# Queries parked with their half-swapped copy, denominators inverted on VectorE in pieces, some transposes on TensorE, SP's queue depth in the schedule

## The chip, the cores and the metric

The kernel runs on one core of a Trainium2 chip. The metric is device time in microseconds. A median of repeated runs is quoted. Profiles are of one execution, so a profile's span can differ from the median by about 0.3%.

Engines: PE is TensorE (PEld its weight loads), DVE is VectorE, ACT is ScalarE, POOL is GpSimd, SP is SyncE, which here only issues transfers.

## The reference

Four layers over a sequence of 2048 rows and 1024 columns, 32 heads of 32: linear attention (A), softmax attention (B), A, B, each with a layer norm before and a residual after. Type bfloat16.

```python
def _A_ref(x, wqkv, w_phi, wo):             # linear attention
    # q, k, v from x @ wqkv, 32 heads
    pq = einsum("bhsd,hdf->bhsf", q, w_phi); pk = ... k ...
    phi_q = concat([softmax(pq), softmax(-pq)]); phi_k = ...
    kv  = einsum("bhsf,bhsd->bhfd", phi_k, v); z = phi_k.sum(s)
    o = einsum(phi_q, kv) / (einsum(phi_q, z) + 1e-6)
    return o @ wo
def _B_ref(x, wqkv, wo):                    # softmax attention
    scores = einsum("bhqd,bhkd->bhqk", q, k) * Dh ** -0.5
    o = softmax(scores) @ v
    return o @ wo
x = x + _A_ref(ln(x)); x = x + _B_ref(ln(x)); x = x + _A_ref(ln(x)); x = x + _B_ref(ln(x))
```

## The kernel before

The kernel records its instructions with its own scheduler. A small clock in Python models each engine, a transfer queue per issuer (`"D"` is SP's, `"P"` GpSimd's) and the buffers, and decides in which order instructions stand on each engine. In the traces each engine runs its list in that order (below, VectorE stands 13.80 us at one instruction while another is queued behind it). So a wrong cost in the model costs no time by itself; it makes an order in which an engine stands in front of something that is not there yet.

An attention unit is a pair of heads times up to 512 queries. TensorE makes scores into `ring`, ScalarE takes the exponential into `E`, TensorE sums `E` against V and against ones into one PSUM accumulator `acc`. VectorE evicts `acc`, or adds it to an earlier partial sum that was parked in DRAM (`pd`). Meanwhile TensorE does background work: projections, feature maps and key-value sums of other rows (`bg`, the `kvacc` accumulator).

The denominators of a finished pair of units go out through DRAM to be spread over 128 partitions, inverted, and fetched back as broadcast rows:

```python
def norm(x0, x1):                            # one pair of units
    ...
    yield ("op", "D", 0.07, lambda e: nc.sync.dma_start(out=dn[0:2, :], in_=a0[64:128:32, :]), 0.0)
    yield dma(dn[2:4, :], a1[0:64:32, :], 20)
    yield dma(rc[:, 0:m], dn[:].rearrange("a (p e) -> (a p) e", e=m), 20)
    yield ("op", "V", 0.2, lambda e: nc.vector.reciprocal(out=rc[:, 0:m], in_=rc[:, 0:m]))
    yield dma(rn[:].rearrange("a (p e) -> (a p) e", e=m), rc[:, 0:m], 20)
    for j in range(4):                       # four broadcast loads of 32 partitions
        ...
    yield tt("P", c_pool(n), o[0:64, ot_cols(u)], a0[0:64, :], a1[0:64, :], ALU.mult)
    yield tt("P", c_pool(n), o[64:128, ot_cols(u)], a1[64:128, :], a0[64:128, :], ALU.mult)
```

A query tile is parked in DRAM as it is, and loaded three times, to get a copy with its halves swapped:

```python
def q_load1(s, src, n, key):
    yield ("op", "D", 0.07, lambda e: nc.sync.dma_start(out=s[:, 0, 0:n], in_=src), 0.0)
    yield ("op", "D", 0.07, lambda e: nc.sync.dma_start(out=s[0:64, 1, 0:n], in_=src[64:128]), 0.0)
    yield dma(s[64:128, 1, 0:n], src[0:64], 256)
```

Normalised rows are transposed by a transfer (`dma_t(xn[u][...], xb2[:])`), and so are the outputs of linear attention. In the scheduler every issue on SP costs 0.07 us and any number of transfers may be in flight.

The softmax here doesn't subtract the row's maximum and nothing guards it: scores larger than these inputs give would overflow.

Of the kernel before, what the change touches and what calls it, by code (L numbers as in the profile page):

```python
# [18 lines left out]
P = 128  # L19
D = 1024  # L20
# [90 lines left out]
class Clock:  # L111


    def __init__(self):
        self.now = 0.0
        self.heap = []
        self.n = 0
        self.busy = {}
        self.keys = {}
        self.kwait = {}  # L120

# [39 lines left out]
    def _op(self, gen, eng, cost, fn, lat=SEM):  # L161
        if isinstance(eng, tuple):
            eng = min(eng, key=lambda e: max(self.busy.get(e, 0.0), self.now))
        if isinstance(cost, dict):
            c = cost[eng]
        else:
            c = cost
        t0 = self.busy.get(eng, 0.0)
        if t0 > self.now + 1e-9:
            self.at(t0, lambda: self._op(gen, eng, cost, fn, lat))  # L170
            return
        fn(eng)
        self.busy[eng] = self.now + c
        if callable(lat):
            lat = lat()
        self.at(self.now + c + lat, lambda: self.step(gen, None))

    def set(self, k):
# [80 lines left out]
def kernel(  # L259
# [64 lines left out]
    st_s = Slots(clk, [sb(f"st{i}", [P, 18], F32) for i in range(4)])  # L324
    sm_s = Slots(clk, [sb(f"sm{i}", [P, 64], F32) for i in range(4)])
    fq_s = Slots(clk, [sb(f"fq{i}", [P, 256], F32) for i in range(2)])
    rc_s = Slots(clk, [sb(f"rc{i}", [P, 16], F32) for i in range(4)])

    def tok(n):
        return Slots(clk, [0] * n)  # L330
# [12 lines left out]

    X = [None] + [[dd(f"x{l}_{t}", [P, D]) for t in range(NT)] for l in (1, 2, 3)]
    xsp = {(l, c): dd(f"xs{l}_{c}", [P, PO, C]) for l in (0, 2) for c in range(NC)}
    qd = {(l, c, g): dd(f"qd{l}_{c}_{g}", [P, C]) for l in (1, 3) for c in range(NC) for g in range(G)}
    pd = {(l, q, p): dd(f"pd{l}_{q}_{p}", [P, C], F32) for l in (1, 3) for q in range(3) for p in range(16)}
    dnd = {n: [dd(f"dn{n}_{i}", [4, n], F32) for i in range(4)] for n in (256, 512)}
    rnd = {n: [dd(f"rn{n}_{i}", [4, n], F32) for i in range(4)] for n in (256, 512)}
    dn_i = [0]  # L350

    def xsrc(l, t):
        if l == 0:
            return A_x[0, t * P:(t + 1) * P, :]
# [9 lines left out]
        return lat  # L364

    def dma(o, i, kb=4):
        return ("op", "D", 0.07, lambda e: nc.sync.dma_start(out=o, in_=i), queue("D", kb))

    def bulk(o, i, kb):
        return ("op", "P", 1.0, lambda e: nc.gpsimd.dma_start(out=o, in_=i), queue("P", kb))  # L370

    def dma_t(o, i):
        return ("op", "D", 0.07, lambda e: nc.sync.dma_start_transpose(out=o, in_=i), queue("D", 400))

    def eng(e):
        return {"V": nc.vector, "S": nc.scalar, "P": nc.gpsimd}[e]
# [17 lines left out]
    def drop(token, b):  # L394
        token.give(0)
        blk.give(b)
# [48 lines left out]
    def ln_tail(u, t, xb, st):  # L445
# [9 lines left out]
        st_s.give(st)  # L455
        clk.start(ln_turn(u, t, xb2))

    def ln_turn(u, t, xb2):
        yield ("key", ("xs", u))
        tt_ = t % 4  # L460
        yield dma_t(xn[u][:, :, tt_ * P:(tt_ + 1) * P], xb2[:])
        drop(t_xn, xb2)
        clk.set(("xt", u, tt_))
        xn_cnt[u] += 1
        if xn_cnt[u] == 4:
            clk.set(("xnT", u))
# [222 lines left out]

    def build_AK(l, c, prs=(0, 1), hs=(0, 1)):  # L690
        u = (l, "K", c)
        if 0 in prs and 0 in hs:
            clk.start(xslot(u, 17))
            clk.start(spill(u))
# [126 lines left out]
    def build_DN(l, c):  # L821
# [38 lines left out]
        def nn(gp, t):  # L860
# [11 lines left out]
            def post(bank, rel, b):  # L872
                ke, kf = ("e", l, c, gp), ("f", l, c, gp)
                n_cnt[ke] = n_cnt.get(ke, 0) + 1
                if n_cnt[ke] == 4:
                    for gi in range(2):
                        drop(t_eq, eq_b[l, c, 2 * gp + gi])
                tmp = b
                t32 = tmp[:].bitcast(F32)
                f = fq_b[l, c, gp]  # L880
                fb = f[:, 192 + 16 * t:192 + 16 * (t + 1)].unsqueeze(2).to_broadcast([P, 16, DH])
                yield tt("V", c_ps(512), t32.rearrange("p (x i) -> p x i", i=DH),
                         bank[:].rearrange("p (x i) -> p x i", i=DH), fb, ALU.mult)
                rel()
                n_cnt[kf] = n_cnt.get(kf, 0) + 1
                if n_cnt[kf] == 4:
                    fq_s.give(f)
                k = (l, 4 * c + t)
                if k not in o_b:
                    o_b[k] = None  # L890
                    o_b[k] = yield from grab(t_o)
                    clk.set(("ob", k))
                    n_cnt[k] = 0
                else:
                    yield ("key", ("ob", k))
                t4 = t32.rearrange("p (g s n) -> p g s n", g=2, s=2)
                yield tt("P" if att_active() else ("V", "P"), {"P": c_pool(256), "V": c_sb(256)},
                         o_b[k][:, gp * 256:(gp + 1) * 256].rearrange("p (g n) -> p g n", g=2),
                         t4[:, :, 0, :], t4[:, :, 1, :], ALU.add)
                drop(t_tmp, tmp)  # L900
                n_cnt[k] += 1
                if n_cnt[k] == 4:
                    oT = yield from grab(t_oT)
                    yield dma_t(oT[:].rearrange("p (g n) -> p g n", g=G), o_b[k][:])
                    drop(t_o, o_b[k])
                    oT_b[k] = oT
                    clk.set(("oT",) + k)
            add(f"n{l}.{c}.{gp}.{t}", [("f", l, c, gp)], None, mms, post, t_tmp)

        ds(0)  # L910
# [5 lines left out]
                ds(gp + 2)  # L916

    def build_AO(l, c):
        for t in range(4):
            tg = 4 * c + t  # L920
            clk.start(x_chain(l, tg, ("oT", l, tg)))
# [14 lines left out]
    def build_BP(l, c, h):  # L936
        u = (l, "B", c)
        if h == 0:
            clk.start(xslot(u, 24))

        def kk(g):
            gl = g % 4
# [13 lines left out]
        def qq(g):  # L956
            gl = g % 4

            def post(bank, rel, b):
                use_xn(u)  # L960
                yield cp(b[:, 0:C], bank[:], C)
                rel()
                yield dma(qd[l, c, g][:], b[:, 0:C], 128)
                drop(t_q, b)
                clk.set(("Qd", l, c, g))
            add(f"q{l}.{c}.{g}", [("xnT", u)], ("bq", g // 4),
# [34 lines left out]
    def q_loader():  # L1001
        for l in (1, 3):
            for vi, (qt, w, ks, part, last, hh) in enumerate(VISITS):
                for g in range(4 * hh, 4 * hh + 4):
                    yield ("key", ("Qd", l, qt // 4, g))
                    s = yield ("take", qs_s)
                    Qt[l, vi, g] = s
                    clk.start(q_load1(s, qd[l, qt // 4, g][:, (qt % 4) * P:(qt % 4 + w) * P], w * P, ("Q", l, vi, g)))

    def q_load1(s, src, n, key):  # L1010
        yield ("op", "D", 0.07, lambda e: nc.sync.dma_start(out=s[:, 0, 0:n], in_=src), 0.0)
        yield ("op", "D", 0.07, lambda e: nc.sync.dma_start(out=s[0:64, 1, 0:n], in_=src[64:128]), 0.0)
        yield dma(s[64:128, 1, 0:n], src[0:64], 256)
        clk.set(key)

    def part_loader():
# [14 lines left out]
    def finish_unit(u):  # L1031
# [19 lines left out]
            clk.set(("part", k, v))  # L1051
            return
        kg = (u.l, u.qt, u.g)
        if not u.fast:
            grp.setdefault(kg, []).append((u, a, token, b))
            if len(grp[kg]) == 2:
                clk.start(norm(*grp.pop(kg)))
            return
        yield from ot_slot(u)
        R = yield from grab(t_R)  # L1060
        r = R[:].bitcast(F32)[:, 0:n]
        n0, d0 = 64 * u.b, 64 * (1 - u.b)
        yield ("op", "V", 0.1 + 0.0065 * n, lambda e: nc.vector.reciprocal(out=r[n0:n0 + 64, :], in_=a[d0:d0 + 64, :]))
        yield tt("V", c_sb(n), ot_ap(u.l, u.q, u.g)[n0:n0 + 64, ot_cols(u)], a[n0:n0 + 64, :], r[n0:n0 + 64, :], ALU.mult)
        drop(t_R, R)
        drop(token, b)
        otb_n[kg] = otb_n.get(kg, 0) + 1
        if otb_n[kg] == 2:
            ot_done(u)

# [17 lines left out]
    def ot_done(u):  # L1088
        for t in range(u.qt, u.qt + u.w):
            clk.set(("ot", u.l, t, u.g))  # L1090
            if u.g == 5:
                clk.set(("ot6", u.l, t))

    def norm(x0, x1):
        u, a0, tk0, b0 = x0
        _, a1, tk1, b1 = x1
        n = u.n
        i = dn_i[0] % 4
        dn_i[0] += 1
        dn, rn = dnd[n][i], rnd[n][i]  # L1100
        rc = yield ("take", rc_s)
        m = n // 32
        yield ("op", "D", 0.07, lambda e: nc.sync.dma_start(out=dn[0:2, :], in_=a0[64:128:32, :]), 0.0)
        yield dma(dn[2:4, :], a1[0:64:32, :], 20)
        yield dma(rc[:, 0:m], dn[:].rearrange("a (p e) -> (a p) e", e=m), 20)
        yield ("op", "V", 0.2, lambda e: nc.vector.reciprocal(out=rc[:, 0:m], in_=rc[:, 0:m]))
        yield dma(rn[:].rearrange("a (p e) -> (a p) e", e=m), rc[:, 0:m], 20)
        rc_s.give(rc)
        for j in range(4):
            dst = (a1[32 * j:32 * (j + 1), :] if j < 2 else a0[32 * j:32 * (j + 1), :])  # L1110
            yield ("op", "D", 0.07, lambda e, j=j, dst=dst: nc.sync.dma_start(
                out=dst, in_=rn[j:j + 1, :].to_broadcast([32, n])), queue("D", 256) if j == 3 else 0.0)
        yield from ot_slot(u)
        o = ot_ap(u.l, u.q, u.g)
        yield tt("P", c_pool(n), o[0:64, ot_cols(u)], a0[0:64, :], a1[0:64, :], ALU.mult)
        yield tt("P", c_pool(n), o[64:128, ot_cols(u)], a1[64:128, :], a0[64:128, :], ALU.mult)
        drop(tk0, b0)
        drop(tk1, b1)
        ot_done(u)

    bo_left = {}

# [304 lines left out]

NBLK = 28
ACT_SLACK = 0.5
NE = 5  # L1430
WINDOW = 60
TRACE = None
# [30 lines left out]
```

## Time and profile before

| | before |
|---|---|
| median | 2660 us |
| PE / ACT / DVE busy | 2292.7 / 2085.9 / 961.8 us |
| issues on SP, in the order of instructions | 1638 |
| PE idle, sum from its timeline | 356 us, 165 of it waiting for exponentials |

The page of before, parts 1 and 2. In part 2 the span is cut into 40 slices and a digit is the busy share in tenths.

```profile
span 2663.0 us, 67052 instructions
## 1 busy us (share of the span) xinstructions
PE 2292.7 (86%) x28268; PEld 913.2 (34%) x28268; DVE 961.8 (36%) x1787; ACT 2085.9 (78%) x2415; POOL 411.2 (15%) x510
...
PE   5878898898999998877878889889889989888787
...
ACT  2433369697999999878986236869797999989998
```

The row of ACT shows the two attentions (the two runs of nines) and the linear layers before each (the twos and threes). Neither PE nor ACT is full everywhere.

I cut the trace at the first and last exponential of each attention. This is the windows view of before for those four stages (start, first attention, boundary, second attention). The columns are stage, length, then busy us of PE, PEld, DVE, ACT, POOL (with counts), granted clock (the share of TensorE's full speed that it was given), DMA share, GB/s.

```profile
0.00:307.70 307.70, 233.75 (x1544) 123.79 (x1545) 201.11 (x382) 97.23 (x177) 75.46 (x118) 0.92 0.56 160
307.70:1437.10 1129.40, 985.93 (x13881) 384.91 (x13882) 397.56 (x711) 989.71 (x1112) 165.80 (x194) 0.93 0.41 117
1437.10:1578.90 141.80, 115.90 (x755) 59.05 (x747) 88.33 (x176) 34.08 (x63) 35.89 (x52) 0.90 0.48 127
1578.90:2650.10 1071.20, 949.54 (x12060) 342.31 (x12060) 269.42 (x513) 964.90 (x1063) 133.47 (x148) 0.87 0.34 100
```

The long stops of PE, from its timeline in before (start, length, what ran, and in brackets the idle time ahead of it and what ended it):

```profile
22.43 3.17 PE L405 MATMUL bg<-slab,xnT 128*128 128x512 bf16 x7 [22.43 <-DMA xnT<-blk]
...
183.49 1.03 PE L405 MATMUL ring<-slab,xnT 128*128 128x512 bf16 x2 [13.10 <-DMA xnT<-blk]
...
1145.37 3.57 PE L405 MATMUL bg<-slab,xnT 128*128 128x512 bf16 x8 [5.62 <-DVE kvacc L388]
...
1232.72 0.59 PE L744 MATMUL bg<-VA,blk 128*128 128x129 bf16 x4 [11.80 <-DVE kvacc L388]
...
1382.67 2.32 PE L402 MATMUL bg<-slab,xnT 128*32 128x512 bf16 x20 [4.99 <-DVE VA L383]
...
1451.89 3.59 PE L405 MATMUL bg<-V,xnT 128*128 128x512 bf16 x8 [8.77 <-DMA xnT<-blk]
```

Three are waits for a transpose by transfer (`xnT<-blk`). The three from 1145 to 1383 us name DVE, which sounds as if DVE were slow. The chain of waits in before, at the longest, says otherwise (start, length, what):

```profile
1213.76 16.39 DMA dn<-blk
...
1230.23 1.79 DMA rc<-dn
...
1232.04 0.20 DVE rc L1106
1232.25 0.43 DVE kvacc L388
...
1232.72 0.59 PE bg L744 x4
```

DVE stands for 13.80 us in front of a reciprocal of 0.2 us, because the transfer on the way to its input (`dn<-blk`) took 16.39 us to land. The key-value addition that PE needs is queued behind it and takes 0.43 us. The other two stops have the same cause: by the DVE timeline it stood 5.68 us (1145) and 4.94 us (1383) at the same small reciprocal just before. The waits view of before sums this (engine, line, releaser: total, times, longest):

```profile
POOL blk L388 <- DMA blk<-rn: 717.8, 88, 21.2
...
DVE rc L1106 <- DMA rc<-dn: 131.9, 41, 13.8
```

The larger number is idle time of an engine that has little to do. The smaller one blocks others.

### The profile page before, as it was taken

The page shows a single profiled execution, that of the slowest core. Times are in us where ns is not written, and L with a number is a line of the kernel's source. Part 1 is how long each engine was busy: PE and PEld are TensorE (multiplying, and loading weights), DVE is VectorE, ACT ScalarE, POOL GpSimd, SP SyncE. Part 2 cuts the span into 40 slices and gives each one's busy share as a digit, 9 for nine tenths or more (in the row PEclk, how much of TensorE's full clock was granted, in tenths as well). Part 3 has the DMA queues.
Part 4 walks back from the last instruction along what each step waited for, and adds up shares of the span by engine and source line. Part 5 has one row for each costly group of instructions (what it writes and reads, how often), then busy time and mean ns, then how long its engine had stood idle before and what let it go on. Part 6 is the DMA issues. An engine that isn't in the chain of part 4 may idle for free.

```text
span 2663.0 us, 67052 instructions
## 1 busy us (share of the span) xinstructions
PE 2292.7 (86%) x28268; PEld 913.2 (34%) x28268; DVE 961.8 (36%) x1787; ACT 2085.9 (78%) x2415; POOL 411.2 (15%) x510
## 2 busy tenths in 40 slices
PE   5878898898999998877878889889889989888787
PEld 2434432333333222333334443333333322223333
DVE  4865641432332234533334665133233221121011
ACT  2433369697999999878986236869797999989998
POOL 3122200100100211221122210010021011122010
PEclk8988999899999889988999899989999987777777
DMA  8364652553253344444134454346335233242111
GB/s 253 86 168 143 162 164 91 149 150 127 72 149 99 112 133 133 134 123 88 43 111 97 130 132 126 102 121 187 104 104 150 93 93 99 88 124 77 32 29 30
DMA packets 280110, 306.69 MB, mean 115 GB/s; under 512 B 147400, under 2 KB 198464, under 8 KB 276736
## 3 DMA queue, kind: packets, MB, share of 16 engines
q1 hardware_dynamic: 253424, 192.29, 26.7%
q0 software_dynamic: 26384, 110.11, 13.1%
q8 instruction: 221, 3.62, 0.6%
q14 instruction: 81, 0.66, 0.1%
HBM read 204.79 MB, written 72.34 MB: 104 GB/s over the span
## 4 chain that ended last, share of the span: by engine, by line
PE 49%; ACT 17%; issue 7%; DMA 4%; DVE 4%; SPq 1%; POOL 0%; ACTq 0%; POOLq 0%; DVEq 0%
PE bg L402 16%; ACT E L1257 15%; PE acc L1313 13%; PE ring L1277 12%; PE ring L405 4%; PE bg L405 3%; DVE blk L388 1%; DMA rc<-dn 1%; DMA xnT<-blk 1%; DMA dn<-blk 1%; ACT blk L705 1%; ACT blk L809 1%; DVE K2b L383 1%; DMA blk<-pd 0%; PE ring L867 0%
## 5 line engine op out<-in xcount | busy, mean ns | idle before, releaser
L1257 ACT ACTIVATE E<-ring 128x1024 bf16<-128x1024 f32 x2048 | 1910.9, 1111 | 197.4 <-PE ring L1277 175.0
L1313 PE MATMUL acc<-E,V 128*32 128x512 bf16 (+1 forms) x5120 | 707.8, 377 | 10.9 <-DVE blk L388 8.6
L1313 PE MATMUL acc<-E,ones 128*32 128x512 bf16 (+1 forms) x5120 | 707.8, 378 | 0.0
L1277 PE MATMUL ring<-Q,K2b 32*128 32x512 bf16 (+1 forms) x2560 | 438.9, 369 | 156.2 <-ACT E L1257 150.0
L1277 PE MATMUL ring<-Q,K2a 32*128 32x512 bf16 (+1 forms) x2560 | 457.8, 371 | 13.6 <-ACT E L1257 13.5
L1313 PEld LDWEIGHTS <-V 128*32 128x32 bf16 x5120 | 204.9, 100 | 315.7 <-issue 286.9
L388 POOL TENSOR_TENSOR blk<-blk,blk 64x512 bf16<-64x512 f32 (+1 forms) x156 | 166.1, 1065 | 773.9 <-DMA blk<-rn 717.8
L1277 PEld LDWEIGHTS <-K2a 32*128 32x128 bf16 x2560 | 123.6, 93 | 427.5 <-issue 417.2
L1277 PEld LDWEIGHTS <-K2b 32*128 32x128 bf16 x2560 | 155.4, 93 | 280.5 <-issue 274.4
L1043 DVE COPY blk<-acc 128x512 f32<-128x512 f32 (+1 forms) x160 | 93.2, 582 | 422.6 <-PE acc L1313 399.4
L388 DVE TENSOR_TENSOR blk<-blk,acc 128x512 f32<-128x512 f32 x128 | 87.6, 684 | 340.3 <-PE acc L1313 322.7
L1313 PEld LDWEIGHTS <-ones 128*32 128x32 bf16 x5120 | 200.8, 100 | 2.1
L402 PE MATMUL bg<-slab,blk 128*32 128x512 bf16 x2596 | 174.3, 386 | 6.8 <-DVE blk L388 5.1
L405 PEld LDWEIGHTS <-xnT 128*128 128x128 bf16 x809 | 80.7, 102 | 163.3 <-DMA xnT<-blk 45.8
L402 PE MATMUL bg<-slab,xnT 128*32 128x512 bf16 x1740 | 124.3, 407 | 14.2 <-ACT blk L705 7.8
L388 DVE TENSOR_TENSOR blk<-blk,bg 128x512 bf16<-128x512 bf16 x110 | 75.3, 685 | 153.5 <-PE bg L402 134.1
L405 PE MATMUL ring<-slab,xnT 128*128 128x512 bf16 x416 | 103.6, 391 | 22.4 <-DMA xnT<-blk 13.1
L388 POOL TENSOR_TENSOR blk<-blk 128x256 bf16<-128x256 f32 x112 | 80.1, 725 | 216.9 <-DVE blk L388 211.9
L402 PEld LDWEIGHTS <-blk 128*32 128x32 bf16 x2968 | 82.6, 98 | 80.9 <-issue 22.8
L710 DVE TENSOR_REDUCE sm<-blk 128x32 f32<-128x1024 bf16 x64 | 77.5, 1211 | 90.7 <-ACT blk L705 86.7
L402 PE MATMUL bg<-xnT,slab 128*32 128x512 bf16 x1424 | 101.0, 397 | 10.4 <-DVE K2b L383 5.8
L405 PE MATMUL bg<-slab,xnT 128*128 128x512 bf16 x301 | 78.9, 409 | 30.0 <-DMA xnT<-blk 22.4
(179 smaller groups left out, 2130.1 us busy)
## 6 DMA issues: line engine op xcount, KB each, us to landing
pd<-blk SPq DMA_DIRECT2D x128, 256.0 KB
blk<-pd SPq DMA_DIRECT2D x128, 256.0 KB
slab<-in_B_wqkv_dram POOLq DMA_DIRECT2D x28, 1024.0 KB, 7.3
Q<-qd SPq DMA_DIRECT2D x256, 64.0 KB
Q<-qd SPq DMA_DIRECT2D x112, 128.0 KB
x<-blk SPq DMA_DIRECT2D x48, 256.0 KB
blk<-rn SPq DMA_DIRECT2D x192, 64.0 KB
blk<-x SPq DMA_DIRECT2D x48, 256.0 KB
```

Source lines behind the costliest of these rows:

```text
L383: eng(e).tensor_copy(out=o, in_=i)
L388: return ("op", e, cost, lambda x: eng(x).tensor_tensor(out=o, in0=a, in1=b, op=op))
L402: nc.tensor.matmul(o[js], lhsT=l[:, js], rhs=r, start=st, stop=sp, tile_position=(0, 32 * j), skip_group_check=True)
L405: nc.tensor.matmul(o, lhsT=l, rhs=r, start=st, stop=sp, skip_group_check=True)
L705: yield ("op", "S", c_act(C), lambda x, s=s: nc.scalar.activation(out=e[:, s * C:(s + 1) * C], in_=bank[:], func=ACT.Exp, scale=1.0 - 2.0 ...
L710: yield ("op", "V", c_sb(1024), lambda x: nc.vector.reduce_sum(out=sm[:, 0:32], in_=e3, axis=AX.X))
L809: yield ("op", "S", c_act(C), lambda x, s=s: nc.scalar.activation(out=e[:, s * C:(s + 1) * C], in_=bank[:], func=ACT.Exp, scale=1.0 - 2.0 ...
L1043: yield ("op", "V", c_ps(n), lambda e: nc.vector.tensor_copy(out=a, in_=acc_t[:, 0:n]))
L1257: yield ("op", "S", c_act(2 * n), lambda x: nc.scalar.activation(out=E[:, :, 0:n], in_=ring_t[buf][:, :, 0:n], func=ACT.Exp, scale=INV_SQR ...
L1277: nc.tensor.matmul(ring_t[bufs[e]][:, j, i * n:(i + 1) * n], lhsT=K2[e][c][u.g // 4][r, u.g % 4, m, :], rhs=u.Q[r, e, 0:n], start=True, st ...
L1313: nc.tensor.matmul(u.acc[r0 + 32 * j:r0 + 32 * j + 32, 0:n], lhsT=lh, rhs=E[:, j, i * n:(i + 1) * n], start=first, stop=final, tile_positi ...
```

## The change

The intent is to relieve SP and its queue, and to let the recorded order know what an issue costs. It has four parts: *schedule*, *queries*, *denominators*, *transposes*.

```diff
 # schedule
+        fly = self.fly.get(eng, ()) if callable(lat) else ()
+        if len(fly) >= 8:
+            t0 = max(t0, fly[-8])
-        return ("op", "D", 0.07, lambda e: nc.sync.dma_start(out=o, in_=i), queue("D", kb))
+        return ("op", "D", 0.45, lambda e: nc.sync.dma_start(out=o, in_=i), queue("D", kb))
-        return ("op", "D", 0.07, ... dma_start_transpose ...)
+        return ("op", "D", 1.3, ... dma_start_transpose ...)
 # queries: parked as [P, 2, C], loaded at once
+                for x in (0, 64):
+                    yield ("op", "V", c_sb(C, 4), lambda e, x=x: nc.vector.tensor_copy(
+                        out=b2[x:x + 64, 1, :], in_=b2[64 - x:128 - x, 0, :]))
-                yield dma(qd[l, c, g][:], b[:, 0:C], 128)
+                yield dma(qd[l, c, g][:], b2, 256)
-        (three loads)
+        yield dma(s[:, :, 0:n], src, n * 0.5)
 # denominators: norm() and its nine transfers are gone
+            yield ("op", "V", c_sb(n, 2), lambda e: nc.vector.tensor_copy(out=r[n0:n0 + 64, :], in_=a[d0:d0 + 64, :]))
+            ...  # the second unit of the pair, when both have copied:
+                for x in range(0, n, P):
+                    yield ("op", "V", 0.1 + 0.0065 * P, lambda e, x=x: nc.vector.reciprocal(
+                        out=r[:, x:x + P], in_=r[:, x:x + P]))
+        yield tt("V" if u.fast else "P", ..., o, a[n0:n0 + 64, :], r[n0:n0 + 64, :], ALU.mult)
 # transposes on TensorE, eight of 128x128 into one bank, then one eviction
+            return (0.062, False, lambda bank, ct, W: nc.tensor.transpose(
+                out=bank.bitcast(BF16)[:, i * P:(i + 1) * P], in_=tr_src[key][0][:, i * P:(i + 1) * P],
+                identity=ident[:]))
+            yield cp(dst, bank.bitcast(BF16).rearrange("p (a n) -> p a n", n=P), 1024)
+TR = {(0, "K", 0), (2, "K", 3), (0, "O", 0), (2, "O", 0), (1, "B", 0), (3, "B", 0)}   # six groups of four tiles
... (cut: the plumbing of keys and buffers)
```

More of the change, by code (lines that the diff above doesn't have):

```diff
@@ L118, in __init__ @@
         self.busy = {}
+        self.fly = {"D": [], "P": []}
         self.keys = {}
@@ L175, in _op @@
             lat = lat()
+            self.fly[eng].append(self.now + c + lat)
         self.at(self.now + c + lat, lambda: self.step(gen, None))
@@ L326 @@
     fq_s = Slots(clk, [sb(f"fq{i}", [P, 256], F32) for i in range(2)])
-    rc_s = Slots(clk, [sb(f"rc{i}", [P, 16], F32) for i in range(4)])
     def tok(n):
@@ L345 @@
     xsp = {(l, c): dd(f"xs{l}_{c}", [P, PO, C]) for l in (0, 2) for c in range(NC)}
-    qd = {(l, c, g): dd(f"qd{l}_{c}_{g}", [P, C]) for l in (1, 3) for c in range(NC) for g in range(G)}
+    qd = {(l, c, g): dd(f"qd{l}_{c}_{g}", [P, 2, C]) for l in (1, 3) for c in range(NC) for g in range(G)}
     pd = {(l, q, p): dd(f"pd{l}_{q}_{p}", [P, C], F32) for l in (1, 3) for q in range(3) for p in range(16)}
-    dnd = {n: [dd(f"dn{n}_{i}", [4, n], F32) for i in range(4)] for n in (256, 512)}
-    rnd = {n: [dd(f"rn{n}_{i}", [4, n], F32) for i in range(4)] for n in (256, 512)}
-    dn_i = [0]
     def xsrc(l, t):
@@ L372, in dma_t @@
     def dma_t(o, i):
-        return ("op", "D", 0.07, lambda e: nc.sync.dma_start_transpose(out=o, in_=i), queue("D", 400))
+        return ("op", "D", 1.3, lambda e: nc.sync.dma_start_transpose(out=o, in_=i), queue("D", 400))
     def eng(e):
@@ L456, in ln_tail, with pe_tr, one, post @@
         clk.start(ln_turn(u, t, xb2))
+    tr_src = {}
+    def pe_tr(key, name):
+        def one(i):
+            return (0.062, False, lambda bank, ct, W: nc.tensor.transpose(
+                out=bank.bitcast(BF16)[:, i * P:(i + 1) * P], in_=tr_src[key][0][:, i * P:(i + 1) * P],
+                identity=ident[:]))
+        def post(bank, rel, b):
+            dst, fin = tr_src[key][1:]
+            yield cp(dst, bank.bitcast(BF16).rearrange("p (a n) -> p a n", n=P), 1024)
+            rel()
+            fin()
+        add(name, [("tr", key)], None, [one(i) for i in range(8)], post)
+    def transpose(key, dst, src, fin):
+        if key in tr_pe:
+            tr_src[key] = (src, dst, fin)
+            clk.set(("tr", key))
+        else:
+            yield dma_t(dst, src[:])
+            fin()
+    tr_pe = set()
     def ln_turn(u, t, xb2):
@@ L460, in ln_turn, with ln_fin @@
         tt_ = t % 4
-        yield dma_t(xn[u][:, :, tt_ * P:(tt_ + 1) * P], xb2[:])
+        yield from transpose((u, tt_), xn[u][:, :, tt_ * P:(tt_ + 1) * P], xb2, lambda: ln_fin(u, tt_, xb2))
+    def ln_fin(u, tt_, xb2):
         drop(t_xn, xb2)
@@ L691, in build_AK @@
         u = (l, "K", c)
+        if u in TR and 0 in hs:
+            for pr in prs:
+                for t in (2 * pr, 2 * pr + 1):
+                    tr_pe.add((u, t))
+                    pe_tr((u, t), f"tr{l}.{c}.{t}")
         if 0 in prs and 0 in hs:
@@ L903, in post, with fin @@
                     oT = yield from grab(t_oT)
-                    yield dma_t(oT[:].rearrange("p (g n) -> p g n", g=G), o_b[k][:])
-                    drop(t_o, o_b[k])
-                    oT_b[k] = oT
-                    clk.set(("oT",) + k)
+                    def fin(oT=oT):
+                        drop(t_o, o_b[k])
+                        oT_b[k] = oT
+                        clk.set(("oT",) + k)
+                    yield from transpose(("o",) + k, oT[:].rearrange("p (g n) -> p g n", g=G), o_b[k], fin)
             add(f"n{l}.{c}.{gp}.{t}", [("f", l, c, gp)], None, mms, post, t_tmp)
@@ L918, in build_AO @@
     def build_AO(l, c):
+        if (l, "O", c) in TR:
+            for t in range(4):
+                tr_pe.add(("o", l, 4 * c + t))
+                pe_tr(("o", l, 4 * c + t), f"to{l}.{c}.{t}")
         for t in range(4):
@@ L939, in build_BP @@
             clk.start(xslot(u, 24))
+            if u in TR:
+                for t in range(4):
+                    tr_pe.add((u, t))
+                    pe_tr((u, t), f"tr{l}.{c}.{t}")
         def kk(g):
@@ L960, in post @@
                 use_xn(u)
-                yield cp(b[:, 0:C], bank[:], C)
+                b2 = b[:].rearrange("p (a n) -> p a n", a=2)
+                yield cp(b2[:, 0, :], bank[:], C)
                 rel()
-                yield dma(qd[l, c, g][:], b[:, 0:C], 128)
+                for x in (0, 64):
+                    yield ("op", "V", c_sb(C, 4), lambda e, x=x: nc.vector.tensor_copy(
+                        out=b2[x:x + 64, 1, :], in_=b2[64 - x:128 - x, 0, :]))
+                yield dma(qd[l, c, g][:], b2, 256)
                 drop(t_q, b)
@@ L1007, in q_loader @@
                     Qt[l, vi, g] = s
-                    clk.start(q_load1(s, qd[l, qt // 4, g][:, (qt % 4) * P:(qt % 4 + w) * P], w * P, ("Q", l, vi, g)))
+                    clk.start(q_load1(s, qd[l, qt // 4, g][:, :, (qt % 4) * P:(qt % 4 + w) * P], w * P, ("Q", l, vi, g)))
     def q_load1(s, src, n, key):
-        yield ("op", "D", 0.07, lambda e: nc.sync.dma_start(out=s[:, 0, 0:n], in_=src), 0.0)
-        yield ("op", "D", 0.07, lambda e: nc.sync.dma_start(out=s[0:64, 1, 0:n], in_=src[64:128]), 0.0)
-        yield dma(s[64:128, 1, 0:n], src[0:64], 256)
+        yield dma(s[:, :, 0:n], src, n * 0.5)
         clk.set(key)
@@ L1053, in finish_unit @@
         kg = (u.l, u.qt, u.g)
-        if not u.fast:
-            grp.setdefault(kg, []).append((u, a, token, b))
-            if len(grp[kg]) == 2:
-                clk.start(norm(*grp.pop(kg)))
-            return
-        yield from ot_slot(u)
-        R = yield from grab(t_R)
-        r = R[:].bitcast(F32)[:, 0:n]
-        n0, d0 = 64 * u.b, 64 * (1 - u.b)
-        yield ("op", "V", 0.1 + 0.0065 * n, lambda e: nc.vector.reciprocal(out=r[n0:n0 + 64, :], in_=a[d0:d0 + 64, :]))
-        yield tt("V", c_sb(n), ot_ap(u.l, u.q, u.g)[n0:n0 + 64, ot_cols(u)], a[n0:n0 + 64, :], r[n0:n0 + 64, :], ALU.mult)
-        drop(t_R, R)
+        n0, d0 = 64 * u.b, 64 * (1 - u.b)
+        yield from ot_slot(u)
+        o = ot_ap(u.l, u.q, u.g)[n0:n0 + 64, ot_cols(u)]
+        if u.fast:
+            R = yield from grab(t_R)
+            r = R[:].bitcast(F32)[:, 0:n]
+            yield ("op", "V", 0.1 + 0.0065 * n, lambda e: nc.vector.reciprocal(out=r[n0:n0 + 64, :], in_=a[d0:d0 + 64, :]))
+        else:
+            if u.b == 0:
+                R = yield from grab(t_R)
+                grp[kg] = R
+                clk.set(("R",) + kg)
+            else:
+                yield ("key", ("R",) + kg)
+                R = grp[kg]
+            r = R[:].bitcast(F32)[:, 0:n]
+            yield ("op", "V", c_sb(n, 2), lambda e: nc.vector.tensor_copy(out=r[n0:n0 + 64, :], in_=a[d0:d0 + 64, :]))
+            clk.set(("Rd", u.b) + kg)
+            if u.b == 0:
+                yield ("key", ("Rd", 1) + kg)
+            else:
+                yield ("key", ("Rd", 0) + kg)
+                for x in range(0, n, P):
+                    yield ("op", "V", 0.1 + 0.0065 * P, lambda e, x=x: nc.vector.reciprocal(
+                        out=r[:, x:x + P], in_=r[:, x:x + P]))
+                clk.set(("Rr",) + kg)
+            yield ("key", ("Rr",) + kg)
+        yield tt("V" if u.fast else "P", c_sb(n) if u.fast else c_pool(n), o, a[n0:n0 + 64, :], r[n0:n0 + 64, :], ALU.mult)
         drop(token, b)
         otb_n[kg] = otb_n.get(kg, 0) + 1
+        if u.fast or otb_n[kg] == 2:
+            drop(t_R, R)
         if otb_n[kg] == 2:
@@ L1092, in ot_done @@
                 clk.set(("ot6", u.l, t))
-    def norm(x0, x1):
-        u, a0, tk0, b0 = x0
-        _, a1, tk1, b1 = x1
-        n = u.n
-        i = dn_i[0] % 4
-        dn_i[0] += 1
-        dn, rn = dnd[n][i], rnd[n][i]
-        rc = yield ("take", rc_s)
-        m = n // 32
-        yield ("op", "D", 0.07, lambda e: nc.sync.dma_start(out=dn[0:2, :], in_=a0[64:128:32, :]), 0.0)
-        yield dma(dn[2:4, :], a1[0:64:32, :], 20)
-        yield dma(rc[:, 0:m], dn[:].rearrange("a (p e) -> (a p) e", e=m), 20)
-        yield ("op", "V", 0.2, lambda e: nc.vector.reciprocal(out=rc[:, 0:m], in_=rc[:, 0:m]))
-        yield dma(rn[:].rearrange("a (p e) -> (a p) e", e=m), rc[:, 0:m], 20)
-        rc_s.give(rc)
-        for j in range(4):
-            dst = (a1[32 * j:32 * (j + 1), :] if j < 2 else a0[32 * j:32 * (j + 1), :])
-            yield ("op", "D", 0.07, lambda e, j=j, dst=dst: nc.sync.dma_start(
-                out=dst, in_=rn[j:j + 1, :].to_broadcast([32, n])), queue("D", 256) if j == 3 else 0.0)
-        yield from ot_slot(u)
-        o = ot_ap(u.l, u.q, u.g)
-        yield tt("P", c_pool(n), o[0:64, ot_cols(u)], a0[0:64, :], a1[0:64, :], ALU.mult)
-        yield tt("P", c_pool(n), o[64:128, ot_cols(u)], a1[64:128, :], a0[64:128, :], ALU.mult)
-        drop(tk0, b0)
-        drop(tk1, b1)
-        ot_done(u)
     bo_left = {}
```

## The prediction

> **What bounds the kernel now.** The page gives PE 2292.7 us busy (86% of 2663.0), ACT 2085.9 (78%), DVE 961.8 (36%). No engine bounds all of it. The 50-us windows show: up to 307 us and from 1430 to 1578 (projections, feature maps) PE is busy 40 to 47 of 50, ACT 10 to 30; in attention (650 to 1100, 1950 to 2650) ACT is busy 48 to 50 (2048 exponentials, 1910.9 us, 0.93 each); between (1100 to 1430) they alternate. PE's idle time in the timeline sums to about 356 us; 165 waits for the exponentials, most of the rest is bank turnover under 1.5 us each. Only the longer stops are in the change's reach: 22.4 us at the start (first transposed tile), 13.1 at 183 (transpose), 5.6 at 1145, 11.8 at 1232 and 5.0 at 1383 (VectorE stuck), 8.8 at 1452 (transpose).
>
> **Removed.** In the order of instructions SP's issues fall from 1638 to 702. Nine denominator transfers per pair of units disappear. Their delay matters through VectorE: the waits show it standing 131.9 us before the small reciprocal (41 times, longest 13.8), other work queued behind; the chain shows that at 1214 (16.4 us of transfer, reciprocal, accumulate, PE). Gain about 22 us from these three stops, 3 more at the end, where broadcast rows are awaited. POOL's 718 us wait for the broadcast costs nothing itself. Q loads go from three transfers to one; they rarely sit on the chain: near 0. With transposes on PE the first matmuls should begin near 14 to 15 us (normalised rows exist at 11.9): 8 us. The 1452 stop: 8 us. The 183 stop has no PE transpose; perhaps half goes by better issue order: 6 us. Sum about 47 us.
>
> **Added.** VectorE: 252 reciprocals of 128x128; the trace has 344 ns for 32 columns and 1747 for 256, so an estimate of 0.93 us each, 234 us; denominator copies, estimated 45 us; half copies 35; evictions of transposes 25, shared with ACT; minus 19. VectorE rises to about 1260 us. In attention windows it is busy 6 to 23 of 50, so this fits, but an eviction may wait up to one reciprocal: 5 to 10 us lost. PE: 192 transposes, mostly in PE-bound stretches, by the 128-column matmuls' spacing of 0.06 to 0.11 us 12 to 20 us. The Trainium skill, "VectorE: DVE Perf Modes", section "The three transpose paths", gives 390 ns for one on TensorE; this trace's back-to-back spacing is smaller, and decides.
>
> **Moved.** About 80 background matmuls of 512 columns move from the first attention to the boundary after it: 15 to 20 us, saved again in the first attention where PE limits it. I count zero.
>
> **Prediction.** 47 minus 12 to 20 minus 5 to 10 is about 25 us: 2632 us, range 2590 to 2662. Faster by over 2% 0.22, within 2% 0.74, slower 0.04.
>
> **What will show it.** First matmul near 14 us; no wait for the small reciprocal, none over 3 us of PE for the key-value accumulator; reciprocals near 0.93 us; DVE busy 1230 to 1290; exponentials still about 1910 us; 1950 to 2650 still ACT-bound, the second attention at most 10 us shorter.
>
> **What would make it wrong.** If the crowded SP queue also delays Q, residual rows and partial sums, more is gained (2600 or below). If the longer boundary is not repaid, or reciprocals delay accumulator evictions by near 1 us at many units, ACT starves and the gain vanishes. A lower granted clock in PE-bound stretches could hide 10 us.

## The result, and the profile after

The median is 2627 us (2624.66 to 2628.97, 4 runs) against 2660 us. All outputs are right. The ratio is 0.9879, 95% interval 0.9857 to 0.9901. All ratios here are the mean time of one kernel's runs over that of the kernel before in the same rounds, so they are not quite the ratios of the medians quoted.

The page of after:

```profile
span 2626.8 us, 65988 instructions
## 1 busy us (share of the span) xinstructions
PE 2304.8 (88%) x28190; PEld 925.2 (35%) x28250; DVE 1262.1 (48%) x2246; ACT 2105.4 (80%) x2443; POOL 426.3 (16%) x519
```

The four stages of after, windows view, columns as above:

```profile
0.00:301.40 301.40, 239.37 (x1635) 130.46 (x1664) 206.79 (x396) 108.42 (x192) 74.76 (x118) 0.95 0.52 154
301.40:1389.20 1087.80, 970.04 (x13558) 375.40 (x13560) 518.41 (x897) 986.82 (x1110) 176.06 (x197) 0.93 0.39 116
1389.20:1551.90 162.70, 139.10 (x952) 75.46 (x962) 107.67 (x208) 45.90 (x81) 40.17 (x58) 0.93 0.35 119
1551.90:2613.80 1061.90, 948.40 (x12021) 340.63 (x12025) 423.87 (x739) 964.21 (x1063) 135.27 (x148) 0.86 0.32 97
```

The first attention lost 41.6 us and the boundary after it gained 20.9: the background work that left one stage stands in the other, as the order had shown. The start lost 6.3 and the second attention 9.3.

PE's timeline of after has no stop for the key-value accumulator above 0.7 us. Its start:

```profile
11.31 1.04 PE L462 MATMUL bg<-ident,blk 128*128 128x128 bf16 x8 [11.31 <-DVE blk L452]
...
16.79 2.39 PE L405 MATMUL bg<-slab,xnT 128*128 128x512 bf16 x8
...
29.69 3.60 PE L405 MATMUL bg<-slab,xnT 128*128 128x512 bf16 x8 [5.33 <-DMA xnT<-blk]
...
39.17 0.39 PE L661 MATMUL bg<-ident,V 128*128 128x128 bf16 x4
```

Projections start 5.6 us earlier than before (16.79 against 22.43). Then PE waits 5.33 us for the *next* rows' transposes, which still go by transfer. The weight fold (`ident,V`) begins at 39.17. In before it began at 40.58:

```profile
40.58 0.38 PE L634 MATMUL bg<-ident,V 128*128 128x128 bf16 x4 [0.88 <-DVE VA L383]
```

Of 5.6 us, 1.4 arrived.

The costliest new group on DVE, by form, in after (count, then busy us and mean ns):

```profile
L1121 DVE RECIPROCAL blk<-blk 128x128 f32<-128x128 f32 x252 | 223.0, 923 | 2.3
...
L1114 DVE COPY blk<-blk 64x512 f32<-64x512 f32 x96 | 50.8, 529 | 3.9
...
L1007 DVE COPY blk<-blk 64x512 bf16<-64x512 bf16 x128 | 43.4, 339 | 3.1
```

DVE does 300 us more and the kernel is faster.

One difference I had named only as a risk. The groups view of ACT gives the exponentials' idle time and its releasers, in before:

```profile
L1257 ACT ACTIVATE E<-ring 128x1024 bf16<-128x1024 f32 x2048 | 1910.9, 1111 | 197.4 <-PE ring L1277 175.0 <-PE acc L1313 20.1 <-ACT E L1257 1.3
```

and in after:

```profile
L1292 ACT ACTIVATE E<-ring 128x1024 bf16<-128x1024 f32 x2048 | 1908.5, 1109 | 152.8 <-PE ring L1312 150.7 <-PE acc L1348 1.0
```

The work is the same; the waits for `acc` fell from 20.1 to 1.0 us. Where they came from is in the chain of waits in before, around one of them (SPq is SP's sequencer, issuing):

```profile
2371.12 0.59 SPq L367
...
2371.81 0.52 SPq L367
...
2372.38 0.42 SPq L1111
...
2372.85 0.41 SPq L1111
2373.31 0.42 SPq L1111
2373.77 0.42 SPq L1111
2374.24 2.73 DMA blk<-pd
2377.06 0.70 DVE blk L388
2377.80 1.05 PE acc L1313 x16
```

The load of the parked partial sum (`blk<-pd`) lands 2.73 us after it is issued, which is quick. It was issued late, because SP was issuing a Q load, a load of denominators and four of their broadcasts (L1111) ahead of it, at 0.4 to 0.6 us each. DVE then adds late, the accumulator comes free late, PE's sums wait, the `E` buffers stay full and ACT stops (5.51 us of idle time up to 2378.30, by its timeline). In the 64 us from 2340, SP issued 92 transfers in before and its issuing took 43 us; in the same stretch of after (2303 to 2367) it issued 22, in 8 us, by the SP timelines.

### The profile page after: what moved, and what is told of

The parts are those of the page before. It is cut to its first block, busy times and chain, and to the rows that moved or that the text cites. A ratio compares the mean times of both kernels' runs of the same rounds, so it can differ in the third digit from the quotient of the medians.

```text
span 2626.8 us, 65988 instructions
## 1 busy us (share of the span) xinstructions
PE 2304.8 (88%) x28190; PEld 925.2 (35%) x28250; DVE 1262.1 (48%) x2246; ACT 2105.4 (80%) x2443; POOL 426.3 (16%) x519
## 5 line engine op out<-in xcount | busy, mean ns | idle before, releaser
L1292 ACT ACTIVATE E<-ring 128x1024 bf16<-128x1024 f32 x2048 | 1908.5, 1109 | 152.8 <-PE ring L1312 150.7
L1312 PE MATMUL ring<-Q,K2a 32*128 32x512 bf16 (+1 forms) x2560 | 459.6, 370 | 10.9 <-ACT E L1292 10.1
L1121 DVE RECIPROCAL blk<-blk 128x128 f32<-128x128 f32 x252 | 223.0, 923 | 2.3
L402 PE MATMUL bg<-slab,xnT 128*32 128x512 bf16 x2076 | 152.2, 414 | 11.0 <-ACT blk L737 9.1
L402 PE MATMUL bg<-xnT,slab 128*32 128x512 bf16 x1596 | 113.0, 399 | 9.6 <-ACT blk L841 4.8
L388 POOL TENSOR_TENSOR blk<-blk 128x256 bf16<-128x256 f32 x102 | 73.5, 730 | 227.3 <-DVE blk L388 226.3
L405 PEld LDWEIGHTS <-xnT 128*128 128x128 bf16 x729 | 71.4, 100 | 101.2 <-issue 18.4
```

The lines of the kernel that those rows point to most:

```text
L388: return ("op", e, cost, lambda x: eng(x).tensor_tensor(out=o, in0=a, in1=b, op=op))
L402: nc.tensor.matmul(o[js], lhsT=l[:, js], rhs=r, start=st, stop=sp, tile_position=(0, 32 * j), skip_group_check=True)
L405: nc.tensor.matmul(o, lhsT=l, rhs=r, start=st, stop=sp, skip_group_check=True)
L1121: yield ("op", "V", 0.1 + 0.0065 * P, lambda e, x=x: nc.vector.reciprocal(out=r[:, x:x + P], in_=r[:, x:x + P]))
L1292: yield ("op", "S", c_act(2 * n), lambda x: nc.scalar.activation(out=E[:, :, 0:n], in_=ring_t[buf][:, :, 0:n], func=ACT.Exp, scale=INV_SQR ...
L1312: nc.tensor.matmul(ring_t[bufs[e]][:, j, i * n:(i + 1) * n], lhsT=K2[e][c][u.g // 4][r, u.g % 4, m, :], rhs=u.Q[r, e, 0:n], start=True, st ...
```

## The experiments

Three theories for the first four runs. A: the gain comes from taking transfers out from in front of VectorE. B: it comes from the schedule that knows the queue. C: it comes from the transposes on TensorE. The stage lengths below are cut as above.

| run | median us | ratio to before | start | first attention | boundary | second attention |
|---|---|---|---|---|---|---|
| before | 2657 to 2661 | 1 | 307.7 | 1129.4 | 141.8 | 1071.2 |
| after | 2627.05 | 0.9879 | 301.4 | 1087.8 | 162.7 | 1061.9 |
| e1 denominators | 2613.64 | 0.9838 | 310.6 | 1081.3 | 157.1 | 1052.2 |
| e2 transposes | 2679.09 | 1.0082 | 310.8 | 1138.9 | 137.6 | 1076.9 |
| e3 schedule | 2640.26 | 0.9940 | 305.8 | 1116.5 | 135.5 | 1066.7 |
| e4 queries | 2639.36 | 0.9934 | 312.9 | 1111.6 | 135.6 | 1067.4 |
| e5 small reciprocal on POOL | 2644.22 | 0.9950 | 309.3 | 1109.7 | 139.2 | 1066.6 |
| e6 after, old denominators | 2652.92 | 0.9971 | 298.5 | 1126.8 | 143.8 | 1075.6 |
| e7 after, 1 of 6 transpose groups | 2637.08 | 0.9916 | 308.4 | 1092.9 | 156.9 | 1059.8 |
| e8 after, order reshuffled | 2625.98 | 0.9867 | 305.2 | 1081.3 | 162.6 | 1062.0 |
| e9 denominators + schedule | 2609.43 | 0.9823 | 301.6 | 1077.2 | 153.1 | 1056.6 |
| e10 denominators + queries | 2614.50 | 0.9844 | 311.0 | 1077.6 | 156.8 | 1052.4 |
| e11 e1, order reshuffled | 2612.76 | 0.9833 | 309.0 | 1081.3 | 159.6 | 1053.0 |
| e12 after, reciprocals whole | 2626.26 | 0.9884 | 299.6 | 1091.5 | 165.0 | 1056.0 |

### e1: the denominators alone

The denominators' part of the diff put into before. With no transpose on TensorE at all the recorder found no schedule (it failed with a weight slab evicted from under a task), so one of the six groups came with it:

```diff
-    def norm(x0, x1): ...            (nine transfers, one small reciprocal)
+    (denominators part of the change)
+TR = {(3, "B", 0)}
```

> The kernel before with the denominators on VectorE alone (without any TensorE transpose the recorder of the kernel does not find a schedule, so the four transposes ahead of the last projection stage are on TensorE too; nothing else is changed). Theory A (the gain comes from taking transfers out from in front of VectorE, which held up the key-value sums and the evictions behind it): 20 to 25 us less than before, ratio 0.990 to 0.993, and the stops of TensorE at about 1145, 1232 and 1383 us are gone. Theory B (the gain comes from the schedule that knows the SP queue): within 5 us of before. Theory C (transposes on TensorE give it): within 5 us of before.

Measured: 0.9838 (0.9795 to 0.9881), some 44 us less than before and faster than the whole change. Theory A's direction holds and its size was too small by half. The stops of PE at 1145, 1232 and 1383 us are gone, and so are ACT's waits for the accumulator:

```profile
L1290 ACT ACTIVATE E<-ring 128x1024 bf16<-128x1024 f32 x2048 | 1909.3, 1122 | 145.8 <-PE ring L1310 144.9
```

Not all of the 44 us need be waits that went away. The page of e1 gives PE 15.4 us less busy time than before, although 32 transposes were added; see "the granted clock" below.

```profile
span 2613.7 us, 66240 instructions
...
PE 2277.3 (87%) x28174; PEld 912.2 (35%) x28174; DVE 1219.6 (47%) x2112; ACT 2089.7 (80%) x2424; POOL 422.9 (16%) x518
```

### e2: the transposes alone

```diff
-        yield dma_t(xn[u][:, :, tt_ * P:(tt_ + 1) * P], xb2[:])
+        (transposes part of the change, all six groups)
```

> The kernel before with the 24 transposes on TensorE alone. Theory A: 5 to 12 us less than before (ratio 0.995 to 0.998), from the stop at 1452 us and a shorter start; the stops at 1145 to 1383 us stay. Theory B: within 5 us. Theory C: 25 us or more less (ratio under 0.991).

Measured: 1.0082 (1.0048 to 1.0117), about 22 us slower. All three theories missed. The stop at 1452 us is gone, and the weight fold starts at 36.46 us instead of 40.58, yet the first exponential comes 3.1 us later and both attentions are longer. PE's busy time rises by 23.7 us, from 2292.7 to 2316.4 us, and the rest of the span falls by only 9. Taken out of the union of PE's busy time, the 192 transposes account for about 13 of the 23.7. The stops behind VectorE stay (6.8 us at 1160, 7.2 at 1242, 5.6 at 1393). Why the second attention is 5.7 us longer was not settled: no transpose on TensorE runs inside it (three groups run before the first attention, three between the two).

### e3: the schedule alone

```diff
-        return ("op", "D", 0.07, ...)
+        return ("op", "D", 0.45, ...)      # 1.3 for a transpose; at most eight in flight
```

> The kernel before, recorded by a schedule that charges 0.45 us for an issue on SP, 1.3 us for a transpose, and lets eight transfers be in flight. No operation is different, only the order. Theory A: within 8 us of before either way, since the nine transfers per pair stay and VectorE still stands before the small reciprocal (100 us or more in all). Theory B: 25 us or more less. Theory C: within 5 us.

Measured: 0.994 (0.9905 to 0.9975), about 17 us less, between A's and B's numbers. No operation differs. VectorE still stands 119.2 us before the small reciprocal, 38 times, but the longest is 6.1 us instead of 13.8; the stop of PE at 183 us (13.1 us) is gone, and that at 1232 is 2.6 us; that at 1145 stays at 4.9. The exponentials' wait for the accumulator did not improve: 32.9 us. Its page shows PE's busy time above that of before, with the same operations:

```profile
span 2637.6 us, 66861 instructions
...
PE 2307.7 (87%) x28160; PEld 913.8 (35%) x28160; DVE 964.3 (37%) x1793; ACT 2084.3 (79%) x2415; POOL 407.9 (15%) x504
```

### e4: the queries alone

```diff
-        (three Q loads)
+        yield dma(s[:, :, 0:n], src, n * 0.5)     # and the half copies ahead of the park
```

> The kernel before with the queries parked with their half-swapped copy, so one Q load instead of three and two more copies on VectorE. Theory A: within 6 us of before. A rival (Q loads crowd the SP queue and delay the denominators' transfers behind them): 10 us or more less, with VectorE's wait before the small reciprocal falling from 132 us to under 80.

Measured: 0.9934 (0.9899 to 0.9969), about 18 us less. The rival is right in direction, wrong in its number: VectorE's total wait is 122.1 us, hardly less, but its longest is 5.6 instead of 13.8 and the stops of PE at 1145 to 1383 us are all under 2.5 us. The sum of the waits did not tell; the longest did. ACT's wait for the accumulator stays at 23.4 us.

### e5: the small reciprocal moved to POOL

```diff
-        yield ("op", "V", 0.2, lambda e: nc.vector.reciprocal(out=rc[:, 0:m], in_=rc[:, 0:m]))
+        yield ("op", "P", 0.5, lambda e: nc.gpsimd.tensor_tensor(
+            out=rc[:, 0:m], in0=rc[:, 0:m], in1=neg1[:, 0:m], op=ALU.pow))
```

> The kernel before with one instruction moved: the small reciprocal of the denominators is taken on GpSimd (a power of minus one), so VectorE no longer stands in front of a transfer. All nine transfers and the full SP queue stay, and VectorE gets no work. Theory A (the stand of VectorE is what cost): 20 us or more less than before, no stop of TensorE over 3 us for the key-value accumulator, and about the gain that the denominators on VectorE gave. Rival A2 (the load on the SP queue is what cost, by delaying everything else): under 8 us less than before.

Measured: 0.995 (0.9925 to 0.9974), about 17 us less. That lies between theory A's 20 and the rival's 8. The longest stop for the key-value accumulator is 2.9 us, so that part of theory A is supported: with VectorE out of the wait the stops go, and the gain is most of their 22 us. It is not the whole of e1's 44, and the order of instructions was recorded anew here too. The exponentials' wait for the accumulator rose to 33.0 us. The run isn't clean: POOL took 2.43 us for each small power where 0.5 was planned, so the loads behind it came later than before.

### e6: after with the old denominators

```diff
-    (denominators part of the change)
+    def norm(x0, x1): ...
```

> The kernel after with the denominators' old path through the transfers. If the parts add (denominators about -40, schedule -16, queries -17, transposes +20 us in the runs of one part each), it is about 2645 us, ratio 0.995. If theory A alone holds, 20 to 30 us above after. Rival (whatever the part, one of three ways to relieve the SP queue suffices): near 2635, ratio 0.99.

Measured: 0.9971 (0.9932 to 1.0009), so 26 us above after by medians, with a wide spread (2637 to 2660). The sum of the single parts (2645) is inside that spread. Stops of PE for the key-value accumulator return (8.9 us at 1140) and ACT's wait for the accumulator is 26.7 us. So the other three parts together gave little without the denominators (8 us by medians, and the interval includes no gain). That is near the sum of their single runs: 17 and 18 us gained, 22 lost. Among these three the parts add, as far as the spread of 22 us tells.

### e7: after with one group of transposes

```diff
-TR = {(0, "K", 0), (2, "K", 3), (0, "O", 0), (2, "O", 0), (1, "B", 0), (3, "B", 0)}
+TR = {(3, "B", 0)}
```

> The kernel after with only one of its six groups of transposes on TensorE, those ahead of the last projection stage; the other twenty go by transfer. If transposes on TensorE cost (+20 us in the run of one part), this is 10 to 25 us faster than after, 2600 to 2617 us, ratio 0.978 to 0.984. If in after's own queue they pay as I predicted, it is 5 to 15 us slower than after, 2632 to 2642.

Measured: 0.9916 (0.9895 to 0.9938), 10 us slower than after by medians. Here the other five groups pay, as I had predicted. In the two profiles, which differ by 4 us only, the start is 7.0 us longer and the first attention 5.1, and the boundary 5.8 shorter. In e2 the groups cost. The sign of this part hangs on what it is combined with.

### e8: a control for the order

```diff
-ACT_SLACK = 0.5
+ACT_SLACK = 0.45
```

> A control for how much a mere reshuffle of the recorded order moves the time: the kernel after with one constant of the recorder (a planned pause of 0.5 us before an exponential of the feature map) set to 0.45; no operation is added or taken away. If the order is robust: within 5 us of after (2622 to 2632). If single runs of one part each carry luck of the order: 10 us or more off, and then no difference under that size between variants may be read as a cause.

Measured: 0.9867 (0.9839 to 0.9895), within 1.1 us of after's median. The stage lengths moved by up to 6.5 us, and partly cancelled. Single stages are thus known to a few us only, totals better.

### e9 and e10: what to put beside the denominators

e9 is e1 plus the schedule part, e10 is e1 plus the queries part.

```diff
 # e9, on e1
+        (schedule part of the change)
 # e10, on e1
+        (queries part of the change)
```

> Denominators on VectorE (with the four transposes it needs) plus the schedule's SP costs, queries in their old form. The run with the denominators alone stood at 0.984, the one with schedule and queries added at 0.992. If the schedule's costs are what takes the gain back: 0.990 to 0.994 (2634 to 2644 us). If the parked query copies do: 0.981 to 0.986.

Measured: 0.9823 (0.9798 to 0.9849), 2609 us, the fastest. The schedule doesn't take the gain back.

> Denominators on VectorE (with the four transposes it needs) plus the parked half-swapped queries, schedule as before. If the parked copies take the gain back: 0.990 to 0.994, with longer idle stretches of ScalarE in the first 350 us of each attention, where Q is awaited. If they are neutral once SP is relieved: 0.982 to 0.986.

Measured: 0.9844 (0.9819 to 0.9869). The parked copies alone don't either. Yet e7, which has both, stands at 0.9916. One thing is visible in e7 and in neither of the two: PE stops 5.06 us for a Q load,

```profile
372.07 0.61 PE L1312 MATMUL ring<-Q,K2a 32*128 32x512 bf16 x2 [5.06 <-DMA Q<-qd]
```

and ACT is idle for 25.7 us ahead of that point, where it is idle 14.4 us in e9 and 19.4 us in e10 at the same place. By that measure it accounts for 6 to 11 of the 23 to 28 us. The pages show where most of the difference stands, but not why: PE is busy for 2301.0 us in e7, 2280.8 in e9 and 2275.9 in e10, for the same operations of PE in another order, at a mean granted clock of 0.906, 0.914 and 0.916. These are the four stages of e9, windows view:

```profile
0.00:301.60 301.60, 231.66 (x1543) 123.27 (x1544) 201.53 (x382) 97.86 (x177) 75.84 (x118) 0.95 0.54 163
301.60:1378.80 1077.20, 960.84 (x13628) 373.66 (x13625) 505.24 (x846) 985.18 (x1108) 174.29 (x194) 0.95 0.37 110
1378.80:1531.90 153.10, 134.32 (x896) 71.12 (x895) 104.03 (x202) 40.77 (x74) 41.56 (x61) 0.93 0.44 136
1531.90:2588.50 1056.60, 945.90 (x12047) 341.85 (x12048) 403.25 (x677) 963.16 (x1063) 135.79 (x149) 0.87 0.32 94
```

Against after it is shorter by 10.6 us in the first attention, 9.6 in the boundary and 5.3 in the second attention, and its start is as short without the start's transposes on TensorE (301.6 against 301.4).

### e11: the control for e1

```diff
-ACT_SLACK = 0.5
+ACT_SLACK = 0.45      # on e1
```

> A control: the run with the denominators alone, the recorder's pause of 0.5 us set to 0.45. If its 0.984 is the work of the change and not of a lucky order: 0.981 to 0.988. If luck: 0.990 or more.

Measured: 0.9833 (0.9808 to 0.9858). e1 was not luck of the order, as far as one reshuffle tells.

### e12: after with the reciprocals whole

```diff
-                for x in range(0, n, P):
-                    yield ("op", "V", 0.1 + 0.0065 * P, ... r[:, x:x + P] ...)
+                yield ("op", "V", 0.1 + 0.0065 * n, lambda e: nc.vector.reciprocal(out=r, in_=r))
```

> The kernel after with the reciprocal of a pair of units taken in one instruction of 512 (or 256) columns instead of pieces of 128. By the 0.923 us of a piece, one takes about 3.5 us, and an accumulator whose eviction comes behind it waits up to that. Theory (pieces are needed): 5 to 20 us slower than after, TensorE's accumulate or ScalarE waiting for evictions more. Rival (VectorE has enough slack and the schedule plans around it): within 5 us of after, ratio 0.986 to 0.990.

Measured: 0.9884 (0.9854 to 0.9914), 0.8 us from after's median. The rival holds: the pieces aren't needed. (The clock was not the same: 0.916 in the mean of its runs, 0.910 in after's. By the estimate below some 6 us could be hidden in that.) ACT waits 3.3 us for the accumulator instead of 1.0. One instruction takes 2.74 us in the mean over both widths.

## Why the prediction was right, and where it was not

The total was predicted at 2632 us and came out at 2627, inside the range. Several readings were right by themselves:

- VectorE's busy time was predicted at 1230 to 1290 us and is 1262.1; a reciprocal at 0.93 us and is 0.923; the exponentials at about 1910 us and are 1908.5; PE's busy time rose by 12.1 us, where 192 transposes were estimated at 12 to 20.
- The three stops behind VectorE are gone. e5 supports their mechanism apart from the rest.
- The longer boundary (20.9 us) was repaid in the first attention, and the second attention is 9.3 us shorter, where at most 10 was said.

But the sum was right partly by luck, because errors in its terms met:

- "Gain about 22 us from these three stops" undersized the denominators. With them alone the kernel is 44 us faster (e1), and inside the change they make 26 us (e6). One missed term stands in the prediction's own list of what would make it wrong: late partial sums. ACT's wait for the accumulator is 20.1 us in before, 22 to 33 us in e2, e3, e4, e5 and e6, and 1.2 us or less in the profiles with denominators on VectorE (after, e1, e7 to e11; 3.3 in e12). So it is about 20 us. That the SP issue stream delays the partial sums is read from the chain and the SP timeline; no run took this cost away by itself. Another may be the granted clock, below.
- "Q loads ... near 0" was wrong. Alone they are worth about 18 us (e4), and the long holds at the small reciprocal are broken up. Beside the denominators they are worth nothing (e10 against e1), as is to be expected when the hold they shorten is gone. The same goes for the schedule's 17 us (e3), of which about 4 are left (e9 against e1, inside the intervals).
- "With transposes on PE the first matmuls should begin near 14 to 15 us: 8 us" was wrong in its consequence. They began at 16.8, and 1.4 us arrived at the weight fold, because the next rows' transposes became the wait.
- "The 183 stop ... perhaps half": it fell from 13.1 to 3.2 us (8.4 in the reshuffled e8, so its size hangs on the order). It is gone in e3 and stays in e1, e2 and e4 (10.9 to 16.3 us), so the schedule's order did that.
- "The 1452 stop: 8 us" came true, but its reason isn't shown. The stop is gone in after, and also in e3 and e4, where the transposes still go by transfer; in e5 it is 2.6 us. There another order was enough.
- "An eviction may wait up to one reciprocal: 5 to 10 us lost" was not seen. Whole reciprocals three times as long on average changed nothing (e12).

The granted clock is a rival that I left out, and no run held it fixed. The prediction named it only as a risk. From the pages and the runs:

| run | granted clock, mean of the runs | PE busy in the profile, us | rest of the span, us |
|---|---|---|---|
| before | 0.901 | 2292.7 | 370 |
| e2 transposes | 0.902 | 2316.4 | 361 |
| e3 schedule | 0.902 | 2307.7 | 330 |
| e4 queries | 0.902 | 2303.1 | 337 |
| e1 denominators | 0.914 | 2277.3 | 336 |
| e9 denominators + schedule | 0.911 | 2280.8 | 321 |
| e10 denominators + queries | 0.912 | 2275.9 | 335 |
| e7 all, 1 of 6 groups | 0.905 | 2301.0 | 330 |
| after | 0.910 | 2304.8 | 322 |

e1, e3 and e4 took about the same out of the rest of the span (34, 40 and 33 us). What sets e1 apart is that PE is busy for 26 to 30 us less than in these two. PE's busy time times the clock of the profile lies between 2069 and 2100 us in all fourteen profiles, so here PE's busy time follows the clock. How much of the total that is worth can only be estimated: among runs of the same kernel (73 runs of 14 kernels, each against its kernel's mean) 0.01 of clock goes with 10.5 us, 95% interval 6.5 to 14.5. By this estimate some 13 of e1's 44 us, and 9 of the change's 33, go with the clock. Whether the order of work raised the clock, or what else did, isn't shown. So "the denominators gave 44 us" is measured, and "the waits that they removed were worth 44 us" is not.

What stays open: why transposes on TensorE cost 22 us alone and save 10 us in the change (by the same estimate 5 of these 10 go with the clock), and why schedule and queries, each harmless beside the denominators, together leave e7 23 to 28 us above e9 and e10, at a lower clock. One control is missing: before itself was never reshuffled. e3, e4 and e5 all gained 17 to 18 us and all recorded the order anew, so a luckier order isn't excluded for them. Against it stands e2, recorded anew as well, which kept stops of 5.6 to 7.2 us behind VectorE. The two controls say that a harmless reshuffle of after or e1 moves a total by about 1 us, so these are not simple noise; the orders differ in many places and I couldn't name one.

The version that the experiments point to is e9: the denominators on VectorE and the schedule's costs, with queries as before and one group of transposes. At 0.9823 (0.9798 to 0.9849) its interval lies below after's 0.9857 to 0.9901. The two weren't timed in the same rounds; each was timed against before.

## What to carry to other kernels

When an engine that runs in order stands in front of a small instruction that needs a transfer, look at the longest of those waits and at what is queued behind, not at the sum and not at the instruction. An issuing engine can stand on the chain though its transfers are quick (here 0.4 to 0.6 us an issue, 43 of 64 us): count the issues in a critical stretch and multiply by the time of one. Before calling a gain the end of a wait, compare the busy time of the limiting engine and the granted clock as well. Parts of a change that relieve the same hold need not add, and together can lose (e7); time each beside the largest one before keeping it.

## What the Trainium skill lacked or had wrong

- "VectorE: DVE Perf Modes", section "The three transpose paths", gives 390 ns for a 128x128 transpose on TensorE, and "TensorE: Matmul & The Clock Gate", section "Part 4: PE-mode transpose", about 275 ns inside a kernel. In after one took 219 ns in the median (314 in e9, where the stretch from 1500 us had a granted clock of 0.76), and eight in a row took 1.04 us from the first's start to the last's end.
- "Advanced Engine Details and Errata", section "X-Bar Transpose (TRN2)", says that transposes by transfer are as fast as regular ones. In after they landed 4.0 us after issue in the median, as loads of residual rows of 256 KB did (4.0); parked stores of 256 KB took 2.3 us. The section leaves out the issuing side: a transpose held SP 1.26 us in the median (longest 12.6 us in before), a load or store of 256 KB 0.32 to 0.42 us.
- No page I read gives the time of a reciprocal on VectorE. Here, on 128 partitions in float32: 344 ns for 32 columns, 923 ns for 128, 1751 ns for 256 and 3349 ns for 512 (the last two in e12).
- No page I read gives the time of a power on GpSimd: 128x16 in float32 took 2.93 us and 128x8 took 1.64 us in e5, where 128x1 took 0.62 us in before.
